# Soft MoE behind an RWKV recurrence on one core: slot sums kept in PSUM, a reordered last chunk, and expert 8 added onto replicated rows

## The chip, the cores and the metric

The kernel runs on one core of one Trainium2 chip. The metric is device time in microseconds (us) for one execution, lower is better. The kernel before took 137.22 us as the median of 13 runs (135.03 to 139.92).

## The reference, cut to what matters

Two stages follow each other. The first is a linear recurrence over 768 steps for each of 4 × 8 heads of width 48; the second takes its output as 3072 tokens of width 384, mixes them into 32 slots (8 experts, 4 slots each), runs each expert's two-layer network on its slots, and mixes the slots back.

```python
for t in range(S):                                   # per batch and head
    cur = einsum('bhd,bhe->bhde', u * k[t], v[t])
    y[t] = einsum('bhd,bhde->bhe', r[t], state + cur)
    state = w * state + einsum('bhd,bhe->bhde', k[t], v[t])
logits = x @ phi                                     # x = y, (3072, 384); phi (384, 32)
d = softmax(logits, axis=0);  slot_input = d.T @ x   # normalised over tokens
for e in range(8):
    slot_out[e] = relu(slot_input[e] @ w1[e]) @ w2[e]   # 384 -> 1024 -> 384
out = softmax(logits, axis=1) @ slot_out             # normalised over slots
```

## The kernel before, in words

The recurrence is computed in chunks. One chunk n is 256 tokens of one batch (two tokens per partition, index j), and there are twelve (nS = 12), three per batch. The order of instructions on every engine is the order of the code: nothing reorders it. What an engine waits for is derived from the tiles that instructions share.

For a chunk, SP loads k, r and v (`load`, L65, three DMAs of 384 KB, four buffers each, issued three chunks ahead). POOL multiplies r and k by powers of w (`mults`, L209, L211) and k by u (L212), two chunks ahead; chunk 0 has this on DVE (L205 to L207). ACT copies r into a PSUM tile rp (`r_copy`, L232), and DVE multiplies k·u by it (`kur`, L238), sums it (`dsum`, L249) and scales v (`dmul`, L256, tile dv). PE transposes r and k (`trans`, L269) and ACT copies them back (L272). `att` (L287) forms the 128 × 128 products of a chunk in two halves j = 0, 1, each in two PSUM banks at_p0 and at_p1, and DVE masks them into at_s (L292). The output y of the chunk accumulates in PSUM from three sources: the diagonal (`y_open`, L302), the state (`inter`, L314, for each half g) and the masked products (`intra`, L354). `state` (L327, L332) and `st_next` (L341) advance the state twice per chunk. ACT copies y to x_t (L365).

Routing follows one chunk behind: `xt` transposes x (L379, L381), `lg` forms logits (L417), `expo` takes exponentials (L426). `disp` (L437), two chunks behind, multiplies x and a column of ones by them into a PSUM tile s_p, which is also the tile of the state products, and DVE adds the result to un_a in SBUF (L441, L443). For each pair of chunks `lexp_t` and `rowsum` (L451 to L461) make the transposed weights LexpT and the reciprocals of their row sums. After the last chunk `last_routing` (L386) does both halves of the routing, un_a is divided by its sums (L533, L535, tile unsiT), and the experts follow in two groups of four (x = 0, 1): `up` (L552, L557, L559), `turn` (transposes of h, L567, L571) and `down` (L578), all with four experts side by side on 32 rows or columns of PE. The expert outputs so_p are copied (L591), replicated onto four groups of 32 rows by a matmul with a selection matrix idrep (L594), and copied again (L595, so_r). Twelve blocks of output follow: matmuls with LexpT (L607), a scaling by DVE or ACT (L613, L615) and a store from SP (L617, L619).

The weights w1 and w2 (25 MB in HBM) are loaded and cast by POOL's DMA queue (`load_w`, L170): 15 pieces of 768 KB, and the last expert's w2 in four of 192 KB. One piece is issued after each of chunks 0 to 8 (W_AT, L469), two inside chunk 9's `mults`, and the rest after them. `fill` issues matmuls whose result nobody reads.

Of the kernel before, what the change touches and what calls it, by code (L numbers as in the profile page):

```python
# [11 lines left out]
def kernel(  # L12
# [12 lines left out]
    nc = tc.nc  # L25
# [51 lines left out]

    wu_row = cst.tile([1, 2, Dm], f32, name="wu_row")
    for t, src in enumerate((w, u)):
        nc.sync.dma_start(out=wu_row[:, t, :], in_=src.flatten()[None, :])  # L80
# [8 lines left out]
    for n in range(3):  # L89
        load(n)  # L90
    warm = cst.tile([P, 1], f32, name="warm")
    nc.vector.memset(warm[:], 1.0)
# [31 lines left out]
    idrep = cst.tile([P, G, ES], bf, name="idrep")  # L124
    hT = cst.tile([P, 2, nF, P], bf, name="hT")
# [26 lines left out]
    un_a = cst.tile([P, (nM + 1) * ES], f32, name="un_a")  # L152
    unsiT = cst.tile([P, nM, 2, ES], bf, name="unsiT")
    csum_r = cst.tile([P, ES], f32, name="csum_r")
# [17 lines left out]
    with tc.tile_pool(name="wk", bufs=2) as wk, \  # L172
# [7 lines left out]
        nc.scalar.activation(out=warm[:], in_=warm[:], func=AF.Ln)  # L180
        nc.scalar.activation(out=logw[:], in_=wu_row[:, 0, :], func=AF.Ln)
        lw_p = ps.tile([P, Dm], f32, name="lw_p", tag="at_p0", padded_shape=[P, nP * P])
# [7 lines left out]
        nc.vector.tensor_copy(u_rep[:].rearrange("p h d -> p (h d)"), u_p[:])  # L190
        nc.vector.memset(idrep[:], 0.0)
        for c in range(XE):
            nc.vector.tensor_copy(idrep[c * ES:(c + 1) * ES, :, c * Spe:ES],
                                  ident[c * ES:(c + 1) * ES, None, c * ES:(c + 1) * ES - c * Spe]
                                  .to_broadcast([ES, G, ES - c * Spe]))

        def mults(n, inner=0):
# [6 lines left out]
            if n == 0:  # L204
                nc.vector.tensor_mul(kk[:, :, :, 0:D], jh(k_l), W_k[:])  # L205
                nc.vector.tensor_mul(rr[:, :, :, 0:D], jh(r_l), W_n[:])
                nc.vector.tensor_mul(ku, ku, u_b)  # L207
            else:
                nc.gpsimd.tensor_mul(rr[:, :, :, 0:D], jh(r_l), W_n[:])  # L209
                load_w(inner)  # L210
                nc.gpsimd.tensor_mul(kk[:, :, :, 0:D], jh(k_l), W_k[:])  # L211
                nc.gpsimd.tensor_mul(ku, ku, u_b)  # L212
# [9 lines left out]
        def r_copy(n, j):  # L222
# [3 lines left out]
            if n == 0 and j == 0:  # L226
                rp = ps.tile([P, H, D], f32, name="rp_first", tag="xl_p", padded_shape=[P, H, D + 8])
            else:
                rp = ps.tile([P, H, D], f32, name="rp") if n == 0 or j == 0 else s["rp"]
            s["rp"] = rp  # L230
            s["rps"] = s.get("rps", []) + [rp]
            nc.scalar.copy(rp[:], jh(loads[n][0])[:, j, :, :])  # L232

        def kur(n, j):
# [3 lines left out]
            nc.vector.tensor_mul(s["ku"][:, j, :, :], s["ku"][:, j, :, :], s["rps"][j][:])  # L238
# [7 lines left out]
        def dsum(n):  # L246
            s = sc[n]
            d = s["rp"][:].rearrange("p h d -> p (h d)")[:, 0:J * H].rearrange("p (j h) -> p j h", j=J)
# [26 lines left out]
        def att(n, j):  # L275
# [6 lines left out]
            at_p = [ps.tile([P, nP, P], f32, name=f"at_p{a}") for a in range(2)]  # L282
# [76 lines left out]
        def x_copy(n):  # L359
            x_t = wk3.tile([P, 2, Dm], bf, name="x_t")  # L360
            if n == nS - 1:
                nc.vector.tensor_copy(x_t[:, 0, :], sc[n]["y"][:, 0, 0:Dm])
                nc.scalar.copy(x_t[:, 1, :], sc[n]["y"][:, 1, 0:Dm])
            else:
                nc.scalar.copy(x_t[:], sc[n]["y"][:, :, 0:Dm])  # L365
            x_of[n] = x_t
            del sc[n]

# [3 lines left out]
        def xt(n):  # L372
# [3 lines left out]
            for g in range(2):  # L376
                for mi in range(nM):
                    o = (g * nM + mi) * P
                    nc.tensor.transpose(xl_p[:, o:o + P], x_of[n][:, g, mi * P:(mi + 1) * P], ident[:])  # L379
# [4 lines left out]
        def last_routing(n):  # L384
# [5 lines left out]
            for g in range(2):  # L390
                for mi in range(nM):
                    nc.tensor.transpose(bank[g][:, mi * P:(mi + 1) * P], x_of[n][:, g, mi * P:(mi + 1) * P], ident[:])
                if g == 0:
                    nc.vector.tensor_copy(xt_s[g][:], bank[g][:, 0:HW])
                else:
                    nc.scalar.copy(xt_s[g][:], bank[g][:, 0:HW])
            fill(2)
            for g in range(2):
                lg_p = bank[g][:, HW:HW + 2 * ES].bitcast(f32)
                for mi in range(nM):  # L400
                    nc.tensor.matmul(lg_p, xt_s[g][:, mi * P:(mi + 1) * P], phi_s[:, mi, :],
                                     start=(mi == 0), stop=(mi == nM - 1), skip_group_check=True)
                nc.scalar.activation(out=le[:, 2 * (n % 2) + g, :], in_=lg_p, func=AF.Exp)
# [4 lines left out]
        def lg(n):  # L408
# [10 lines left out]
            if n % 2 == 0:  # L419
                le_of[n // 2] = wk.tile([P, G, ES], bf, name="Lexp")  # L420
# [8 lines left out]
        def disp(n, s_p):  # L429
# [3 lines left out]
            for g in range(2):  # L433
                q = 2 * (n % 2) + g
                for mi in range(nM + 1):
                    lhs = ones[:] if mi == nM else x_of[n][:, g, mi * P:(mi + 1) * P]
                    nc.tensor.matmul(s_p[:, mi * ES:(mi + 1) * ES], lhs, le[:, q, :],  # L437
                                     start=(g == 0 and mi == 0), stop=(g == 1), skip_group_check=True)
            w = (nM + 1) * ES
            if n == 0:  # L440
                nc.vector.tensor_copy(un_a[:], s_p[:, 0:w])  # L441
            else:
                nc.vector.tensor_add(un_a[:], un_a[:], s_p[:, 0:w])  # L443
# [19 lines left out]
        def fill(count):  # L463
            pad = ps.tile([P, H, D], f32, name="pad", tag="rp")
            for _ in range(count):
                nc.tensor.matmul(pad[:].rearrange("p h d -> p (h d)"), ident[:], w1_all[:, 0, 0, 0:Dm],
                                 start=True, stop=True, skip_group_check=True)

        W_AT = [1] * 9 + [32] * 5  # L469
# [11 lines left out]
        for n in range(nS):  # L481
# [6 lines left out]
            s_now = ps.tile([P, nP * D2], f32, name="s_p")  # L488
            disp(n - 2, s_now)
            sc[n]["s"] = s_now  # L490
            trans(n + 1, "rr")
            if n == nS - 1:
# [157 lines left out]
```

The softmax here doesn't subtract the row's maximum and nothing guards it: scores larger than these inputs give would overflow.

## Time and profile before

| What | us |
|---|---|
| median of 13 runs | 137.22 |
| the profiled execution | 135.03 |
| its span on the core | 133.2 |
| PE busy | 99.1 (74%) |
| DVE busy | 97.9 (73%) |
| POOL busy | 78.6 (59%) |
| ACT busy | 77.2 (58%) |
| DMA: 31.78 MB moved | mean 238 GB/s |

In the profile PE is the matmul engine and PEld its weight loads; DVE, ACT and POOL are the vector, scalar and general engines; SP issues DMAs. A row such as `DVE at_s L292` names engine, tile written and line. An arrow `x<-y` reads "x written from y". In the chain of waits each line is a start, a length and what ran; in the timeline a bracket gives the idle time ahead of an instruction and who ended it. Bytes of the cast weights are counted as they arrive, in bf16.

### The profile page before, as it was taken

How to read it: one execution, taken by the hardware profiler on the slowest of the kernel's cores; microseconds unless marked ns; L12 is line 12 of the kernel's file. 1: busy time of each engine (PE TensorE's matmuls, PEld its weight loads, DVE VectorE, ACT ScalarE, POOL GpSimd, SP SyncE). 2: the span in 40 equal slices, each digit the busy share in tenths (PEclk: the TensorE clock that was granted, in tenths of full speed). 3: DMA queues.
4: the chain of work that ended last, by engine and by line, in shares of the span. 5: the costliest groups of instructions: out<-in, count | busy, mean ns of one | idle time of the engine just before them, and what ended most of it. 6: DMA issues, size and time to landing. Idle time of an engine off the chain costs nothing.

```text
span 133.2 us, 4106 instructions
## 1 busy us (share of the span) xinstructions
PE 99.1 (74%) x1727; PEld 69.4 (52%) x1727; DVE 97.9 (73%) x195; ACT 77.2 (58%) x130; POOL 78.6 (59%) x63
## 2 busy tenths in 40 slices
PE   0826898987589977997698868899868879779100
PEld 0325585865468665685467646686745545332000
DVE  6699997999787798868988996967895342277600
ACT  4848675776766577665948675765732422057500
POOL 5008999999999999189396894999370000000000
PEclk9999999999955599559959995555899999997555
DMA  1999999999999999999999999999999999119993
GB/s 22 319 323 325 325 325 290 244 261 260 232 267 240 259 248 239 238 231 247 184 211 290 192 243 281 170 198 207 208 206 203 206 202 200 20 45 412 406 406 153
DMA packets 51351, 31.78 MB, mean 238 GB/s; under 512 B 38386, under 2 KB 46836, under 8 KB 51332
## 3 DMA queue, kind: packets, MB, share of 16 engines
q0 software_dynamic: 11600, 12.63, 56.8%
q1 hardware_dynamic: 39316, 18.88, 49.2%
q8 instruction: 13, 0.21, 0.6%
q10 hardware_dynamic: 416, 0.00, 0.2%
q14 instruction: 6, 0.05, 0.1%
HBM read 39.38 MB, written 4.72 MB: 331 GB/s over the span
## 4 chain that ended last, share of the span: by engine, by line
DMA 26%; ACT 20%; PE 16%; DVE 15%; issue 9%; POOL 9%; DVEq 0%; ACTq 0%; POOLq 0%
DMA w_all<-in_moe_w_dram 14%; DMA r_l<-in_r_dram 7%; POOL w_all L170 5%; DVE at_s L292 5%; DMA out_dram<-o_s 5%; ACT t_kk L272 4%; ACT rp L232 4%; PE t_p L269 4%; DVE k_l L238 3%; ACT x_t L365 3%; ACT v_bf L219 3%; ACT xt_s L381 2%; PE at_p L287 2%; PE xl_p L379 1%; PE s_p L332 1%
## 5 line engine op out<-in xcount | busy, mean ns | idle before, releaser
L292 DVE TENSOR_TENSOR at_s<-at_p,mask 128x512 bf16<-128x512 f32 x48 | 30.9, 685 | 9.0 <-PE at_p L287 8.9
L209 POOL TENSOR_TENSOR rr<-r_l,W_n 128x768 bf16<-128x768 f32 x11 | 20.4, 1854 | 16.6 <-DMA r_l<-in_r_dram 16.5
L212 POOL TENSOR_TENSOR k_l<-k_l,u_rep 128x768 f32<-128x768 f32 x11 | 19.9, 1811 | 0.9
L211 POOL TENSOR_TENSOR kk<-k_l,W_k 128x768 bf16<-128x768 f32 x11 | 19.9, 1811 | 0.0
L232 ACT COPY rp<-r_l 128x384 f32<-128x384 f32 x23 | 11.2, 486 | 11.8 <-DVE k_l L238 11.6
L272 ACT COPY t_rr<-t_p 128x1024 bf16<-128x1024 bf16 x11 | 11.1, 1012 | 11.3 <-PE t_p L269 11.2
L287 PE MATMUL at_p<-t_rr,t_kk 64*64 64x128 bf16 x384 | 15.4, 269 | 2.7 <-DVE at_s L292 1.3
L170 POOL DMA_DIRECT2D w_all<-in_moe_w_dram x19 | 15.6, 830 | 2.1 <-DMA w_all<-in_moe_w_dram 2.1
L272 ACT COPY t_kk<-t_p 128x1024 bf16<-128x1024 bf16 x12 | 12.1, 1005 | 2.2 <-PE t_p L269 2.1
L332 PE MATMUL s_p<-v_bf,kk 64*128 64x96 bf16 x160 | 13.1, 238 | 0.0
L238 DVE TENSOR_TENSOR k_l<-k_l,rp 128x384 f32<-128x384 f32 x23 | 12.6, 549 | 0.6
L287 PEld LDWEIGHTS <-t_kk 64*64 64x64 bf16 x384 | 9.4, 131 | 6.5 <-issue 4.8
L332 PEld LDWEIGHTS <-kk 64*128 64x128 bf16 x160 | 9.6, 113 | 5.7 <-issue 5.7
L256 DVE TENSOR_TENSOR dv<-v_bf,rp 128x768 bf16<-128x768 bf16 x12 | 11.4, 953 | 1.5 <-ACT t_kk L272 0.5
L341 DVE TENSOR_TENSOR st<-s_p,wm 128x384 bf16<-128x384 f32 x20 | 11.0, 552 | 1.5 <-PE s_p L332 1.3
L269 PE MATMUL t_p<-ident,kk 128*128 128x128 bf16 x96 | 10.0, 267 | 2.6 <-DVE kk L205 2.6
L249 DVE TENSOR_REDUCE rp<-k_l 128x16 f32<-128x768 f32 x12 | 11.5, 958 | 0.3
L365 ACT CAST x_t<-y_p 128x768 bf16<-128x768 f32 x11 | 8.9, 805 | 3.4 <-PE y_p L354 3.4
L381 ACT COPY xt_s<-xl_p 128x768 bf16<-128x768 bf16 x11 | 8.8, 800 | 2.7 <-PE xl_p L379 2.7
L615 ACT ACTIVATE o_s<-o_p,rsum_r 128x384 f32<-128x384 f32 x12 | 6.4, 585 | 6.6 <-PE o_p L607 4.4
L354 PE MATMUL y_p<-v_bf,at_s 64*128 64x48 bf16 x384 | 9.8, 192 | 0.3 <-issue 0.3
L269 PEld LDWEIGHTS <-kk 128*128 128x128 bf16 x96 | 7.4, 120 | 5.0 <-DVE kk L205 3.7
(105 smaller groups left out, 177.9 us busy)
## 6 DMA issues: line engine op xcount, KB each, us to landing
w_all<-in_moe_w_dram POOLq DMA_DIRECT2D x15, 768.0 KB, 9.8
k_l<-in_k_dram SPq DMA_DIRECT2D x12, 384.0 KB, 6.0
r_l<-in_r_dram SPq DMA_DIRECT2D x12, 384.0 KB, 6.1
v_l<-in_v_dram SPq DMA_DIRECT2D x12, 384.0 KB, 9.0
out_dram<-o_s SPq DMA_DIRECT2D x11, 384.0 KB, 4.1
w_all<-in_moe_w_dram POOLq DMA_DIRECT2D x4, 192.0 KB, 20.4
out_dram<-o_s SPq DMA_DIRECT2D x2, 192.0 KB, 1.9
phi_f<-in_moe_phi_dram POOLq DMA_DIRECT2D x1, 48.0 KB, 4.7
```

The source lines that it names most:

```text
L170: nc.gpsimd.dma_start(out=dst, in_=src)
L209: nc.gpsimd.tensor_mul(rr[:, :, :, 0:D], jh(r_l), W_n[:])
L211: nc.gpsimd.tensor_mul(kk[:, :, :, 0:D], jh(k_l), W_k[:])
L212: nc.gpsimd.tensor_mul(ku, ku, u_b)
L232: nc.scalar.copy(rp[:], jh(loads[n][0])[:, j, :, :])
L238: nc.vector.tensor_mul(s["ku"][:, j, :, :], s["ku"][:, j, :, :], s["rps"][j][:])
L269: nc.tensor.transpose(t_p[:, q, :, j, :], s[nm][:, j, 2 * q:2 * q + 2, :].rearrange("p h d -> p (h d)"), ident[:])
L272: nc.scalar.copy(t_s[:], t_p[:])
L287: nc.tensor.matmul(at_p[a][g * HF:(g + 1) * HF, q, :], kT[sl, q, g, j, :], rT[sl, q, g, :, :].rearrange("p j c -> p (j c)"), start=True, s ...
L292: nc.vector.tensor_mul(s["at"][:, a, j, :, :], at_p[a][:], mask[:, j, None, :].to_broadcast([P, nP, P]))
L332: nc.tensor.matmul(s_p[:, q * D2:(q + 1) * D2], s["kk"][sl, j, 2 * q:2 * q + 2, :].rearrange("p h d -> p (h d)"), s["v"][sl, j, 2 * q:2 * ...
L365: nc.scalar.copy(x_t[:], sc[n]["y"][:, :, 0:Dm])
```

## The change

1. The first chunk's loads are issued ahead of the two small loads of w and u, which move from SP to ACT's DMA queue; the first activation table is loaded right behind them. 30 unread matmuls (`spin`) are put around PE's first products. The copy u_rep moves behind the products of chunk 0, and idrep is built much later.
2. `disp` accumulates over all chunks in one PSUM tile (rpun, which also holds rp) and the additions into un_a go. The sums stay unscaled: unsiT is a plain copy, and the reciprocal of the sums (csum_r, turned to a column csum_c by a matmul) scales so_r at the end instead, in two halves, DVE's and ACT's.
3. POOL issues two weight pieces after chunk 5 instead of one.
4. The last chunk has its own order: the second half of `att` uses the bank t_p beside at_p0, `intra` stands ahead of the second `inter`, the second transposes and row sums (`last_weights`, `last_sums`) move between `turn` and `down`, and y is copied into two tiles, ACT's and DVE's.
5. Expert 8 is left out of `down(1)`. Its h is copied into four row groups (hL), and its eight matmuls add onto the replicated rows sr_p. The memsets of hT (POOL before) and hL are on DVE.

```diff
+    load(0)
-        nc.sync.dma_start(out=wu_row[:, t, :], in_=src.flatten()[None, :])
+        nc.scalar.dma_start(out=wu_row[:, t, :], in_=src.flatten()[None, :])
+    nc.scalar.activation(out=warm[:], in_=warm[:], func=AF.Ln)
...
+        rpun = ps.tile([P, 512], f32, name="rpun")
+        un_p = rpun[:, Dm:Dm + (nM + 1) * ES]
+        rp_v = rpun[:, 0:Dm].rearrange("p (h d) -> p h d", h=H)
...
-                    nc.tensor.matmul(s_p[:, mi * ES:(mi + 1) * ES], lhs, le[:, q, :],
-                                     start=(g == 0 and mi == 0), stop=(g == 1), skip_group_check=True)
-                nc.vector.tensor_add(un_a[:], un_a[:], s_p[:, 0:w])
+                    nc.tensor.matmul(un_p[:, mi * ES:(mi + 1) * ES], lhs, le[:, q, :],
+                                     start=(n == 0 and g == 0 and mi == 0), stop=(n == nS - 1 and g == 1),
+                                     skip_group_check=True)
...
-        W_AT = [1] * 9 + [32] * 5
+        W_AT = [1] * 5 + [2] + [1] * 3 + [32] * 5
...
+        n = nS - 1
+        att(n, 0)
+        disp(n - 2)
+        xt(n - 1)
+        y_open(n)
+        sc[n]["s"] = ps.tile([P, nP * D2], f32, name="s_p")
+        state(n, 0)
+        att(n, 1)
+        inter(n, 0)
+        lg(n - 1)
+        expo(n - 1)
+        fill(4)
+        st_next(n, 0)
+        intra(n)
+        inter(n, 1)
+        x_last(n, 0)
+        x_last(n, 1)
+        fill(1)
+        disp(n - 1)
+        last_routing(n)
+        disp(n)
+        fill(3)
...
+        nc.vector.tensor_copy(unsiT[:], un_p[:, 0:nM * ES].rearrange("p (m s) -> p m s", m=nM)[:, :, None, :]
+                              .to_broadcast([P, nM, 2, ES]))
+        nc.vector.reciprocal(csum_r[:], un_p[0:1, None, nM * ES:(nM + 1) * ES].to_broadcast([1, G, ES]))
...
+        nc.vector.memset(hT[:], 0.0)
+        nc.vector.memset(hL[:], 0.0)
...
         up(0)
         up(1)
         turn(0)
+        selection()
+        last_weights()
         down(0)
         turn(1)
+        last_sums()
         down(1)
...
+        nc.vector.tensor_copy(so_b[:], so_p[:])
+        nc.tensor.matmul(sr_p[:], idrep[:].rearrange("p g t -> p (g t)"), so_b[:], start=True, stop=False,
+                         skip_group_check=True)
+        for fi in range(nF):
+            nc.tensor.matmul(sr_p[:], hL[:, fi, :, :].rearrange("p g t -> p (g t)"), w2_all[:, E - 1, fi, :],
+                             start=False, stop=(fi == nF - 1), skip_group_check=True)
+        nc.vector.tensor_scalar_mul(so_r[:, 0:Dm // 2], sr_p[:, 0:Dm // 2], csum_c[:])
+        nc.scalar.activation(out=so_r[:, Dm // 2:Dm], in_=sr_p[:, Dm // 2:Dm], func=AF.Copy, scale=csum_c[:])
```

## The prediction

> **What bounds the kernel now.** I read the page first (slices, chain), then the chain in order of time, three-microsecond windows, the timeline of the end and POOL's waits. The slices say that the 16 DMA engines are busy from 3 to 113 us and that no compute engine is:
>
> ```profile
> PE 99.1 (74%) x1727; PEld 69.4 (52%) x1727; DVE 97.9 (73%) x195; ACT 77.2 (58%) x130; POOL 78.6 (59%) x63
> ...
> DMA  1999999999999999999999999999999999119993
> ```
>
> The chain in order of time (start, length, what) shows which transfer ends last, and what follows it:
>
> ```profile
> 72.49 9.20 DMA r_l<-in_r_dram
> ...
> 96.50 18.93 DMA w_all<-in_moe_w_dram
> 115.43 0.04 issue
> 115.47 0.50 PE so_p L578 x2
> 115.99 0.57 DVE so_b L591
> 116.56 0.04 issue
> 116.60 0.34 PE sr_p L594
> 116.96 0.57 DVE so_r L595
> 117.57 0.61 PE o_p L607 x8
> ```
>
> The last slice of expert 8's w2 lands at 115.43; two matmuls, a copy, a matmul and a copy later, at 117.57, the output starts. From there to 133.2 the DMA writes 4.72 MB at about 413 GB/s; nothing there changes, so I price everything at the first output matmul. But compute is nearly as late. In the timeline the second `down` starts at 113.54 and sits idle only 0.33 us before its last pair:
>
> ```profile
> 107.99 2.77 PE L552 MATMUL h_p<-w_all,unsiT 128*32 128x512 bf16 x48 [0.35 <-DVE rsum_r L461]
> ...
> 113.54 2.41 PE L578 MATMUL so_p<-w_all,hT 128*32 128x384 bf16 x32
> 115.47 0.09 PEld L578 LDWEIGHTS <-hT 128*32 128x32 bf16 x1 [0.33 <-issue]
> ```
>
> So two chains end together: transfers (A) and compute (B). A saving counts only as far as both have it. The windows (last two columns: DMA share, GB/s) show how full A is:
>
> ```profile
> 39.00:42.00 3.00, 2.58 (x31) 2.02 (x30) 2.77 (x5) 2.73 (x4) 2.98 (x3) 0.50 1.11 210
> 63.00:66.00 3.00, 1.60 (x55) 1.26 (x54) 2.78 (x5) 3.00 (x5) 0.84 (x2) 1.00 0.98 189
> 84.00:87.00 3.00, 2.57 (x30) 2.24 (x27) 2.92 (x7) 2.03 (x5) 2.92 (x3) 0.50 0.97 156
> 93.00:96.00 3.00, 3.00 (x68) 2.50 (x67) 2.89 (x5) 2.06 (x3) 1.36 (x2) 0.82 1.12 207
> ```
>
> Loads of r, k, v alone run at 325 GB/s (9 to 21 us), weights alone at 207 (counted as bf16). Only 63 to 66 and 84 to 87 lie below both: 3 × (1 − 156/207) = 0.74 us of empty engines in the second, and about 1.0 in the first, whose mix of loads and weights would run near 280 (the rate of 69 to 72). POOL issues the weights between its products, and it waits for loads:
>
> ```profile
> POOL rr L209 <- DMA r_l<-in_r_dram: 16.5, 5, 7.6
> ```
>
> **What the Trainium skill says.** "DMA: Bandwidth & Descriptors", section Queues, rings and completion order: each engine goes round-robin, packet by packet, over the queues that have work, so a load beside a weight crawls. The trace agrees: at 39 to 42 us, with v_l issued at 37.54 still outstanding, the rate is that of weights alone. "PSUM — Partial Sum Buffer", section PSUM bank collisions raise a hardware error: two engines may not touch one bank and quadrant at once, reads included. The trace agrees: ACT's x_t copy (L363, 103.64) starts only when DVE's copy of the other half of y_p (L362, 103.05 for 0.56) is done. "VectorE: DVE Perf Modes", section Zero memsets can be issued as uint32: a memset takes a cycle per element; here 128 take 0.17 us, 384 take 0.38, so 0.82 ns each.
>
> **The start.** SP issues two wu_row DMAs at 0.74 and 1.15 ahead of k_l at 1.44; now k_l goes first: A −0.70. ACT issues wu_row instead, and its w_pd issues (0.89 for two) move between the two table steps, so logw goes from 3.23 to about 4.2 and W_k from 5.47 to 6.0–6.4 (the second table load, 1.28, now follows logw in the open). That costs nothing, because kk of chunk 0 (L205) waits in DVE's queue behind u_rep, idrep's memset and its four copies until 8.25. Without these it starts near 7.3. u_rep (0.56) returns ahead of ku. First kur: 11.08 to about 10.7, B −0.4. If POOL needed W_n earlier this would show, but POOL starts at 10.39 on a load. The spins lie in PE's idle time before 9.29; no row shows 30 such matmuls, the pads' 0.16 to 0.24 each bound them at 7 us, of which at most 1 us could push the transposes; I take 0.
>
> **Slot sums.** The 11 adds and one copy into un_a (0.28 each, 3.3 us of DVE) go. In the loop they are not in the chain by name: it runs over ACT's copies, kur and at_s, and DVE waits for PE's at_p right after them. Bounds for ten chunks: 0 and −2.8; I take 0. disp now shares rp's bank, so its first weight load waits for DVE's dv, which stands ahead of st (today's wait) in DVE's queue: no later than now. r_copy waits for disp, but t_rr's copy ahead of it waits for the transposes behind disp anyway. Queued behind disp: those transposes.
>
> **The extra weight at n=5.** POOL issues a second 768 KB weight at 53.96, ahead of rr for chunk 8, which waits for its load until 57.10 anyway: 0.94 us hidden. It adds no bytes, only order. One weight is 786 KB, 3.84 us at 205 GB/s. For: the hole at 63 to 66 fills, A up to −1.0. Against: r_l of chunk 9, landing at 65.6 now, waits behind one or two weights more, 3.9 to 7.7 us. ku of chunk 9 ends at 71.08 and is first used by kur at 76.97: slack 5.9. I take 0, with −1.0 and +1.8 (7.7 − 5.9) as ends.
>
> **The last chunk (B).** Today att(11,0) starts at 97.10 and `up` at 107.99: 10.9 us. New order from the same start and rows: disp(9), xt, y_open and state fill PE until 99.5, where today's PE waits for at_s; second att to 99.9; at_s on DVE to 101.25; st_next to 101.8; intra from 101.4, inter to 102.35; x copies one after the other (0.48, 0.56) to 103.4; transposes and copies to 104.15; logits, exp to 104.7; disp to 105.1; one copy (0.36) replaces add, reciprocal and product (0.29 + 0.35 + 0.36), and the last LexpT and row sums leave: `up` at 105.55. B −2.4, with −1.5 and −3 as ends.
>
> **Up, turn, down (B).** Counted from `up`. DVE first does csum_r (128 elements; rows of 4 and 32 give 0.18 and 0.35, so 0.9) and the memsets of hT and hL (1024 and 512 words: 0.9 + 0.45), so h_s is 0.34 later than PE needs it; two transposes 0.28; `selection` 0.9 hides under down(0); hL copy 0.2 and nine small matmuls 0.35 ahead of down(1), which starts at 6.5 where it is 5.55 now. Its 24 matmuls run three abreast (1.5, to 8.0), so_b 0.6, then nine full ones (0.33 + 8 × 0.16 = 1.6), to 10.2. so_r's halves, 0.4 each, are not parallel: in the built program ACT's half waits for DVE's (both read sr_p): to 11.15. Today 9.58. B +1.57. POOL's memset of hT (1.83) leaves a queue that is empty by then: 0.
>
> **The tail (A).** After the last landing: 0.04 + two matmuls 0.50 + 0.02 + 0.40 + 0.03 + 0.40 + 0.05 = 1.44, where it is 2.14. A −0.70.
>
> **Sum.** A: −0.70 − 0.70 = −1.40. B: 105.55 − 0.4 + 11.15 = 116.3 against 117.57, −1.25. The later decides: −1.25. The profiled execution took 135.03 us, 133.2 of it span; it is the fastest of the 13. Applied to the median 137.22: 136.0. What made the slower ones slow I can't see; a lower TensorE clock would weigh on B.
>
> **Rivals.**
> Likeliest, 0.42: 136.0, own range 135.2 to 136.9.
> Faster, 0.25: the extra weight fills the hole without hurting chunk 9 (A −2.4), and the missing adds shorten ten chunks by 0.1 each (B −2.3): 134.9, down to 133.8. For it: DVE is the busiest engine of the loop beside ACT. Against: the adds are not in the chain.
> Slower, 0.18: the extra weight starves POOL. rr of chunk 9 starts 7 us late; the loads then all finish early, and a weight every 5.4 us of products (three times 1.81) can't fill engines that need one every 3.84. One gap of 2.7 us opens near 85: A −1.40 + 2.7 = +1.3, 138.5. It decides once chunk 9's load is over 5.9 us later than now. For it: POOL already waits there five times. Against: 16.5 us of such waits leave the engines full today.
> No change, 0.15: the new order gains only 1.2 in the last chunk, because ACT's copies and not PE's waits set it; B −0.05: 137.2.
>
> **Numbers.** The measurement tells about 0.5% (0.7 us) from no change. Faster by more: most of the first case and all of the second, 0.60; same 0.21; slower 0.19. Range 134.0 to 138.2.
>
> **What would show it.** First k_l issue near 0.74; `up` 8.5 us after the last att(·,0) starts; first output matmul 1.4 to 1.5 us after the last weight lands; so_r's ACT half behind DVE's; no hole near 63 us. Wrong if chunk 9's rr starts after 71 or DMA share falls under 0.9 near 85.

## The result, and the profile after

| | kernel before | kernel after |
|---|---|---|
| median, us | 136.68 (48 runs, 134.72 to 140.10) | 138.51 (11 runs, 137.3 to 141.5) |
| the profiled execution, us (its span) | 135.03 (133.2) | 138.13 (136.4) |
| ratio after to before | | 1.0154, 95% interval 1.0111 to 1.0198 |

Slower by 1.5%, where −0.9% was forecast. Ratios compare undisturbed executions with undisturbed ones, so a median over all executions can stand a little off its ratio, and the one execution of each kernel that has a profile was a disturbed one in e5, e12 and i1 below.

The page of the kernel after, engines, chain shares, and the group of rr on POOL (GpSimd):

```profile
PE 105.9 (78%) x1759; PEld 75.6 (55%) x1759; DVE 97.4 (71%) x186; ACT 77.7 (57%) x131; POOL 77.0 (56%) x62
...
POOL 32%; issue 21%; PE 18%; DMA 9%; ACT 8%; DVE 4%; SPq 2%; POOLq 0%; DVEq 0%; ACTq 0%
...
L214 POOL TENSOR_TENSOR rr<-r_l,W_n 128x768 bf16<-128x768 f32 x11 | 20.6, 1877 | 20.1 <-DMA r_l<-in_r_dram 20.0
```

POOL, which has 44% of the span free, now holds the largest share of the chain, and its waits for r_l have grown from 16.5 to 20.0 us. The timeline of POOL in the kernel after shows where (start, length, what, and in brackets the idle time ahead of it):

```profile
55.41 1.81 POOL L170 DMA_DIRECT2D w_all<-in_moe_w_dram  x2
58.21 1.81 POOL L214 TENSOR_TENSOR rr<-r_l,W_n 128x768 bf16<-128x768 f32 x1 [0.99 <-DMA r_l<-in_r_dram]
...
63.62 0.94 POOL L170 DMA_DIRECT2D w_all<-in_moe_w_dram  x1
73.76 1.80 POOL L214 TENSOR_TENSOR rr<-r_l,W_n 128x768 bf16<-128x768 f32 x1 [9.20 <-DMA r_l<-in_r_dram]
```

Two weights are issued at 55.41 and a third at 63.62; rr of chunk 9 starts at 73.76, where it was 65.62: 8.1 us later. A window of the kernel after (POOL's column is 0.00; DMA share and GB/s last), and its DMA queues in the same three microseconds (packets, MB, share of the engines; q0 carries the weights, q1 the loads), show who had the engines meanwhile:

```profile
69.00:72.00 3.00, 2.72 (x28) 2.01 (x26) 2.39 (x6) 1.93 (x4) 0.00 (x0) 0.50 1.25 204
```

```profile
q0 software_dynamic: 533, 0.41, 86.3%
q1 hardware_dynamic: 535, 0.20, 38.8%
```

The total of 204 GB/s is also that of weights alone, but the loads do move: one packet of a load (384 bytes) goes for each packet of a weight (768 bytes). So loads get a third of the bytes, about 68 GB/s where they have 325 alone, and one load of 393 KB takes 5.8 us. SP had issued this r_l at 56.98: it was over 15 us under way. In e1 below, with one weight, it is issued at 56.95 and rr starts at 66.25; the weight's own part of the delay is then 7.5 us.

Chunk 9's ku then reaches kur at 79.25 instead of 76.97, and the last chunk's first scores start at 99.05 instead of 97.10. But DVE waits for ku only 0.51 us:

```profile
79.25 0.55 DVE L243 TENSOR_TENSOR k_l<-k_l,rpun 128x384 f32<-128x384 f32 x1 [0.51 <-POOL k_l L217]
```

DVE itself was late, because PE was. The same window in the kernel after, in the kernel before and in e1 (PE's busy time and matmuls first; third from the end is the granted clock, the share of its full speed that PE gets):

```profile
67.00:80.00 13.00, 12.55 (x180) 9.25 (x178) 9.01 (x16) 7.13 (x12) 6.14 (x5) 0.50 1.18 244
```

```profile
67.00:80.00 13.00, 10.77 (x226) 7.94 (x223) 11.54 (x22) 9.22 (x15) 11.01 (x8) 0.88 1.21 235
```

```profile
67.00:80.00 13.00, 9.45 (x237) 7.44 (x234) 11.57 (x20) 9.46 (x17) 10.63 (x7) 1.00 1.23 232
```

From first scores to first scores, a chunk takes 7.19 us in e1 at full clock (71.71 to 78.90); in the kernel after chunk 7 takes 9.12 (65.63 to 74.75), 1.6 more than before, and no product of chunk 9 is used in it. So in this profile the late load is 0.5 us of the 1.95, at most the 1.0 that chunk 8 loses, and the rest goes with the half clock.

The timeline from the last chunk to `up`:

```profile
107.72 0.36 DVE L544 CAST unsiT<-rpun 128x192 bf16<-128x192 f32 x1 [0.87 <-PE rpun L445]
107.99 0.93 DVE L546 RECIPROCAL csum_r<-rpun 1x128 f32<-1x128 f32 x1
...
108.98 1.26 PE L594 MATMUL h_p<-w_all,unsiT 128*32 128x512 bf16 x20 [0.81 <-DVE csum_r L546]
```

`up` waits not for unsiT, which it reads, but for csum_r, which it doesn't: both read the PSUM bank of rpun, and the h_p tiles take its place. `up` at 108.98 is 9.93 us after the last chunk's start (10.89 before, 8.45 forecast). The end, in the same view:

```profile
117.17 1.46 PE L645 MATMUL sr_p<-w_all,hL 128*128 128x384 bf16 x8
...
118.66 0.42 DVE L647 TENSOR_SCALAR so_r<-sr_p,csum_c 128x192 bf16<-128x192 f32 x1 [1.71 <-PE sr_p L645]
...
119.12 0.42 ACT L648 ACTIVATE so_r<-sr_p,csum_c 128x192 bf16<-128x192 f32 x1 [4.35 <-DVE so_r L647]
...
119.59 0.85 PE L660 MATMUL o_p<-so_r,LexpT 32*64 32x384 bf16 x16 [0.96 <-ACT so_r L648]
```

The eight matmuls of the eighth expert run in one stretch: the last weight, landed at 116.84, was there before them. So compute (chain B) ended last, at 119.59 against 117.57, and the difference adds up: +1.95 at the last chunk's start, −0.96 to `up`, +1.03 from `up` to the output = +2.02. From there to the landing of the last store it took 15.7 us, against 14.6; the kernels below took 14.6 to 15.9, and I have no cause for that 1.1. The last weight, too, landed late: 116.84 against 115.43, though the first load was issued at 0.74 as forecast.

To see where transfers (chain A) lost time, I worked out from the packets of the trace, stretch by stretch, how much transfer time is missing: the length of the stretch less the loads' bytes at 325 GB/s and the weights' at 205. I call it the gap. From 17 to 25 us it is 0.51 us before and 1.36 after; from 54 to 60 it is 0.33 and 1.51. The second difference is not the extra weight's: e1, with one weight, has 1.19 there, and e2, with two, 0.35.

### The profile page after: what moved, and what is told of

It is laid out like the page before. It is cut to its first block, busy times and chain, and to the rows that moved or that the text cites. A ratio compares the mean times of both kernels' runs of the same rounds, so it can differ in the third digit from the quotient of the medians.

```text
span 136.4 us, 4158 instructions
## 1 busy us (share of the span) xinstructions
PE 105.9 (78%) x1759; PEld 75.6 (55%) x1759; DVE 97.4 (71%) x186; ACT 77.7 (57%) x131; POOL 77.0 (56%) x62
## 4 chain that ended last, share of the span: by engine, by line
POOL 32%; issue 21%; PE 18%; DMA 9%; ACT 8%; DVE 4%; SPq 2%; POOLq 0%; DVEq 0%; ACTq 0%
POOL kk L216 12%; POOL k_l L217 9%; POOL rr L214 6%; DMA out_dram<-o_s 5%; POOL w_all L170 5%; DMA r_l<-in_r_dram 4%; SPq L72 2%; PE so_p L623 2%; PE h_p L594 2%; PE t_p L274 2%; ACT x_t L367 2%; PE pad L470 1%; ACT t_kk L277 1%; PE s_p L338 1%; DVE k_l L243 1%
## 5 line engine op out<-in xcount | busy, mean ns | idle before, releaser
L298 DVE TENSOR_TENSOR at_s<-at_at_p,mask 128x512 bf16<-128x512 f32 x47 | 30.3, 685 | 11.3 <-PE at_at_p L293 11.2
L237 ACT COPY rpun<-r_l 128x384 f32<-128x384 f32 x23 | 11.2, 486 | 12.4 <-DVE k_l L243 12.0
L293 PE MATMUL at_at_p<-t_rr,t_kk 64*64 64x128 bf16 x376 | 15.2, 274 | 2.5 <-DVE at_s L298 1.2
L338 PE MATMUL s_p<-v_bf,kk 64*128 64x96 bf16 x160 | 13.9, 247 | 0.0
L338 PEld LDWEIGHTS <-kk 64*128 64x128 bf16 x160 | 10.2, 117 | 5.9 <-issue 5.9
L243 DVE TENSOR_TENSOR k_l<-k_l,rpun 128x384 f32<-128x384 f32 x23 | 12.6, 549 | 1.2 <-POOL k_l L217 0.5
L261 DVE TENSOR_TENSOR dv<-v_bf,rpun 128x768 bf16<-128x768 bf16 x12 | 11.4, 953 | 1.1
L254 DVE TENSOR_REDUCE rpun<-k_l 128x16 f32<-128x768 f32 x12 | 11.5, 955 | 0.3
L274 PE MATMUL t_p<-ident,kk 128*128 128x128 bf16 x96 | 10.7, 280 | 0.0
L320 PE MATMUL y_p<-st,t_rr 128*128 128x96 bf16 x80 | 8.7, 248 | 1.6 <-DVE st L347 1.5
L224 ACT CAST v_bf<-v_l 128x768 bf16<-128x768 f32 x12 | 9.9, 829 | 0.0
L274 PE MATMUL t_p<-ident,rr 128*128 128x128 bf16 x88 | 9.7, 278 | 0.3 <-POOL rr L214 0.3
```

The costliest lines, as they stand in the source:

```text
L254: nc.vector.tensor_reduce(d, s["ku"], axis=mybir.AxisListType.X, op=ALU.add)
L274: nc.tensor.transpose(t_p[:, q, :, j, :], s[nm][:, j, 2 * q:2 * q + 2, :].rearrange("p h d -> p (h d)"), ident[:])
L293: nc.tensor.matmul(at_p[a][g * HF:(g + 1) * HF, q, :], kT[sl, q, g, j, :], rT[sl, q, g, :, :].rearrange("p j c -> p (j c)"), start=True, s ...
L298: nc.vector.tensor_mul(s["at"][:, a, j, :, :], at_p[a][:], mask[:, j, None, :].to_broadcast([P, nP, P]))
L338: nc.tensor.matmul(s_p[:, q * D2:(q + 1) * D2], s["kk"][sl, j, 2 * q:2 * q + 2, :].rearrange("p h d -> p (h d)"), s["v"][sl, j, 2 * q:2 * ...
```

## The experiments

Two questions. First, what made it slower: the theory (T1) is the slower rival of the prediction, the second weight at chunk 5; its rivals are csum_r ahead of `up` and the longer steps behind it (T2 in the recorded texts), and the transfers that landed late. Second, once T1 stood: why undoing the weight doesn't bring the forecast gain. Ratios are to the kernel before, with 95% intervals; each kernel had 22 executions unless another number is given.

| kernel | ratio | interval |
|---|---|---|
| e1, after with one weight | 1.0015 | 0.9984 to 1.0047 |
| e2, before with two weights (6) | 1.0149 | 1.0082 to 1.0215 |
| e3, after with late csum_r | 1.0060 | 1.0022 to 1.0099 |
| e4, e1 and e3 together | 1.0017 | 0.9986 to 1.0049 |
| e5, e4 with the old start (6) | 1.0168 | 1.0098 to 1.0238 |
| e6, e4 with five buffers (6) | 1.0112 | 1.0039 to 1.0185 |
| e7, after with five buffers | 1.0083 | 1.0044 to 1.0122 |
| e8, e4 without the eighth expert's change | 1.0065 | 1.0024 to 1.0105 |
| e9, e4 without spins | 0.9973 | 0.9940 to 1.0005 |
| e10, before with the new start (6) | 1.0109 | 1.0042 to 1.0176 |
| e11, before with the eighth expert's change | 0.9964 | 0.9920 to 1.0008 |
| e12, before with both (6) | 1.0225 | 1.0147 to 1.0302 |
| h1, e10 with squarings on POOL (14) | 1.0028 | 0.9964 to 1.0092 |
| h2, e9 with squarings on POOL | 0.9928 | 0.9893 to 0.9963 |
| h3, e12 with squarings on POOL (14) | 0.9983 | 0.9938 to 1.0028 |
| h4, e9 with the old start | 1.0018 | 0.9968 to 1.0067 |
| i1, h2 with two weights | 1.0038 | 1.0005 to 1.0071 |
| i2, h2 with spins | 0.9984 | 0.9946 to 1.0022 |

**e1: the second weight taken out of the kernel after.**

```diff
-        W_AT = [1] * 5 + [2] + [1] * 3 + [32] * 5
+        W_AT = [1] * 9 + [32] * 5
```

> The changed kernel with one weight piece after chunk 5, as before (W_AT), and nothing else undone. Theory T1 (the second piece keeps chunk 9's loads waiting, POOL starts chunk 9's rr at 73.8 in place of 65.6, and chunks 9 to 11 start 1.95 us late): rr of chunk 9 back near 65 to 66, last chunk's att at 96.7 to 97.2, first output matmul at 117.0 to 117.4, time 0.2 to 0.6 us under the kernel before. Theory T2 (the delay is made in the new last chunk and the longer up, turn and down): last att moves by less than 0.5 us and the time stays 1.3 us or more over the kernel before.

Measured 1.0015: the loss of 1.5% is gone. rr of chunk 9 starts at 66.25. The gain that was expected on top didn't come: the output follows the last weight, which lands at 116.55, by 1.49 us.

**e2: the second weight alone, put into the kernel before** (the same line the other way round).

> The kernel before with the second weight piece after chunk 5 and nothing else. T1: rr of chunk 9 at 72 to 75, last att 1.5 to 2 us late, time 1.5 to 2.5 us over the kernel before. T2: within 0.5 us of the kernel before, since nothing at the end is changed.

Measured 1.0149, which is the whole of the loss. POOL's timeline in this kernel repeats the pattern:

```profile
53.08 1.82 POOL L170 DMA_DIRECT2D w_all<-in_moe_w_dram  x2
...
62.35 0.94 POOL L170 DMA_DIRECT2D w_all<-in_moe_w_dram  x1
71.18 1.80 POOL L209 TENSOR_TENSOR rr<-r_l,W_n 128x768 bf16<-128x768 f32 x1 [7.89 <-DMA r_l<-in_r_dram]
```

So T1 holds from both sides as to the time: the weight is enough for the loss, and without it there is none. As to the path it holds only in part. In this profile DVE waits 0.68 us for POOL's ku at chunk 11, the last chunk starts 0.75 us late (97.85), and then it takes 13.38 us to `up` instead of 10.89, with the granted clock at 0.50 for 10 of them.

**e3: the reciprocal of the kernel after moved off `up`'s way.** The bank is released by a copy of 32 sums, and csum_r is made in `selection`.

```diff
-        nc.vector.reciprocal(csum_r[:], un_p[0:1, None, nM * ES:(nM + 1) * ES].to_broadcast([1, G, ES]))
+        csum_x = cst.tile([1, ES], f32, name="csum_x")
+        nc.vector.tensor_copy(csum_x[:], un_p[0:1, nM * ES:(nM + 1) * ES])
...
         def selection():
+            nc.vector.reciprocal(csum_r[:], csum_x[0:1, None, :].to_broadcast([1, G, ES]))
```

> The changed kernel with csum_r's 0.93 us reciprocal taken out from between unsiT and up: a copy of the 32 sums (about 0.1) stands there, and the reciprocal follows in selection, under down(0). Both theories: up starts 0.8 us sooner after unsiT. T1: that is a part of the loss only, first output matmul at 118.7 to 118.9, the time still 1.0 to 1.5 us over the kernel before. T2: the time falls by 0.8 us and up to 1.3 with what follows it, to within 0.6 us of the kernel before.

Measured 1.0060, 0.9% under the kernel after. Its timeline, both weights still in:

```profile
104.19 0.36 DVE L544 CAST unsiT<-rpun 128x192 bf16<-128x192 f32 x1 [0.87 <-PE rpun L445]
104.47 0.17 DVE L547 COPY csum_x<-rpun 1x32 f32<-1x32 f32 x1
...
104.70 0.83 PE L596 MATMUL h_p<-w_all,unsiT 128*32 128x512 bf16 x12
```

The copy takes 0.17 us where the reciprocal took 0.93, and `up` comes 8.07 us after the last chunk's first scores. That the time falls while the second weight is in, and (next) not when it is out, fits compute as the later chain. This profile, though, is of the fastest of the 22 executions (135.56 us), and in it the second weight does no harm: rr of chunk 9 starts at 67.68, DVE doesn't wait for POOL in chunks 9 to 11, and the output follows the last weight by 1.49 us. So two weights do not starve chunk 9 in every execution.

**e4: both.**

> Both edits: one weight piece after chunk 5, and csum_r late. If the two losses add (1.95 and 0.8), the compute chain ends about 2.8 us earlier than in the changed kernel, and the transfers (116.2 for the first output matmul) decide: 1.0 to 1.5 us under the kernel before. If transfers were the real end already, no more than 0.3 us better than the run with one weight piece alone.

Measured 1.0017, no better than e1. The timeline of its end says why:

```profile
114.81 1.14 PE L647 MATMUL sr_p<-w_all,hL 128*128 128x384 bf16 x6
116.46 0.48 PE L647 MATMUL sr_p<-w_all,hL 128*128 128x384 bf16 x2 [0.52 <-DMA w_all<-in_moe_w_dram]
...
117.91 0.52 PE L662 MATMUL o_p<-so_r,LexpT 32*64 32x384 bf16 x8 [0.96 <-ACT so_r L650]
```

Here A decides: PE waits for the last weight, landed at 116.42, and the output starts 1.49 us later. The tail is as forecast (1.44), but the weight lands 1.0 us later than before instead of 0.7 earlier: the second question.

**e5 and e6: does the early start vanish in four load buffers?** e5 puts the old start back into e4 (w and u on SP ahead of the first load). e6 gives r and k five buffers, and the cast v and x two in place of three.

```diff
-            t = loads[n][x]
+            t = loads[n][x] = ld.tile([P, H, J, D], f32, name=("r_l", "k_l", "v_l")[x], bufs=(5, 5, 4)[x])
...
-            load(n + 3)
+            load(n + 3, (2,))
+            load(n + 4, (0, 1))
```

> The kernel with one weight per chunk and the late reciprocal, but with the start of the kernel before: SP issues the rows w and u ahead of the first load, and the table load stands where it stood, so the first load goes out near 1.4 us instead of 0.74. If the four load buffers give the early start back between 17 and 25 us (SP then waits for a buffer sooner and longer), the last weight lands where it did (116.4 us of a profile), the gap at 17 to 25 us shrinks from 1.3 us of lost transfer to about 0.5, and the time is 136.9 (within 0.3). If the early start reaches the end of the transfers, the time rises by 0.6 to 0.8, to 137.6.

> The kernel with one weight per chunk and the late reciprocal, with five buffers for r and k in place of four, their loads issued four chunks ahead, the load of v three ahead as before, and two buffers in place of three for the cast v and x. If four buffers give the early start back, and cause other gaps in the transfers, the gap at 17 to 25 us goes, the last weight lands 0.7 to 1.2 us sooner (115.2 to 115.7), and since it ends last there, the time falls to 135.7 to 136.2. If SP's waits for buffers cost no transfer (the queue holds enough), it stays at 136.9, and the end is set by the rate at which weights and loads share the engines.

Neither came as written. The gap at 17 to 25 us was 1.14 in e5 and 1.31 in e6: it is there with the old start and with five buffers, so the four buffers don't make it. The times, 1.0168 and 1.0112, rest on four and two executions; they are above e4, and for e6 against its own profile, whose last weight lands at 115.11. I leave e6's time unexplained.

**e7: five buffers in the kernel after, two weights left in.**

> The kernel after, with two weights at chunk 5, with the five buffers alone added. If the extra weight delays chunk 9 because its loads wait for a buffer, rr of chunk 9 starts near 66 to 68 us again instead of 73.8 and the time falls to 136.5 to 137.2. If the extra weight delays it by taking the DMA engines while the loads are already issued, rr of chunk 9 still starts after 71 and the time stays within 0.5 of 138.5.

Measured 1.0083, 0.7% under the kernel after, with intervals that touch: between the two answers. rr of chunk 9 starts at 68.25, as the first one said, in a profile of the fastest execution (135.69 us). That the fifth buffer does it is not shown. Its r_l was issued at 54.31, ahead of the second weight (55.76), where the kernel after issues it behind (56.98 and 56.34); but e3, with four buffers, issues it at 53.91 and has rr at 67.68, and e2 at 53.10 with rr at 71.18.

**e8: e4 without the eighth expert's change.**

```diff
+            for group in ((0, 1, 2), (3,)) if x == 1 else ((0, 1, 2, 3),):
                 for fi in range(nF):
-                for c in range(XE - x):
+                    for c in group:
...
-        for fi in range(nF):
-            nc.tensor.matmul(sr_p[:], hL[:, fi, :, :].rearrange("p g t -> p (g t)"), w2_all[:, E - 1, fi, :],
-                             start=False, stop=(fi == nF - 1), skip_group_check=True)
```

> The kernel with one weight per chunk and the late reciprocal, with the eighth expert undone: down(1) runs experts 5 to 7 and then the eighth into so_p, and so_b and the replication follow the last weight; no hL. Where transfers end last, the step from the last weight's landing to the first output matmul goes from 1.49 us back to about 2.1 to 2.3, and the time rises by 0.6 to 0.8, to 137.6. If compute ends last anyway, the time stays at 136.9 or falls by up to 0.3, since the two copies into hL and its memset go.

Measured 1.0065, 0.5% over e4. In its timeline the copy and the replication are behind the last weight again, which landed at 115.28:

```profile
115.32 0.48 PE L620 MATMUL so_p<-w_all,hT 128*32 128x384 bf16 x2 [0.23 <-DMA w_all<-in_moe_w_dram]
...
116.45 0.32 PE L639 MATMUL sr_p<-so_b,idrep 128*128 128x384 bf16 x1 [0.65 <-DVE so_b L638]
...
117.73 0.85 PE L654 MATMUL o_p<-so_r,LexpT 32*64 32x384 bf16 x8 [0.96 <-ACT so_r L642]
```

2.45 us from landing to output against e4's 1.49. The step works where A decides.

**e9: e4 without the 30 spin matmuls.**

```diff
-        spin(12)
...
-        spin(18)
```

> The kernel with one weight per chunk and the late reciprocal, without the 30 spin matmuls at the start. In the profiles of after and of every kernel made from it the first 16 KB instruction fetch stands at 16.0 to 18.5 us instead of 20.4, and a gap of 1.1 to 1.4 us of lost transfer follows in 17 to 25 us, where before has 0.5. If the spins' instructions bring the fetch forward and that makes the gap, the fetch goes back to about 20, the gap falls to 0.5 to 0.7, and the time falls by 0.5 to 0.8, to 136.2. If the spins have nothing to do with it, the gap stays above 1.1 and the time at 136.9 (within 0.3).

Measured 0.9973, 0.4% under e4 with intervals that overlap; the fetch came at 18.7 us and the gap was 0.98. That the fetch makes the gap fell with e10, where it comes at 21.7 and the gap is 2.1.

**e10, e11, e12: the start and the eighth expert's change alone in the kernel before.**

```diff
+    load(0)
...
-        nc.sync.dma_start(out=wu_row[:, t, :], in_=src.flatten()[None, :])
+        nc.scalar.dma_start(out=wu_row[:, t, :], in_=src.flatten()[None, :])
+    nc.scalar.activation(out=warm[:], in_=warm[:], func=AF.Ln)
...
-    for n in range(3):
+    for n in range(1, 3):
         load(n)
```

> The kernel before with the new start alone: load(0) first, the rows w and u on ScalarE, the table load behind them. If the earlier start reaches the end where transfers end last, the time is 0.5 to 0.8 below before, ratio 0.995. If it is given back between 17 and 25 us by something that comes with the start itself, the time stays at that of before, ratio 1.000, and the gap there grows from 0.5 to 1.2 us.

> The kernel before with the eighth expert's change alone: hL, down(1) over experts 5 to 7, so_b and the replication ahead of the last weight, the eighth expert's eight matmuls onto sr_p; so_r still copied whole by DVE. Transfers and compute end together before, so if the prediction's step is right the time from the last weight's landing to the first output matmul falls from 2.14 us to 1.5 and the time by 0.5 to 0.8, ratio 0.995. If compute ends last, it stays within 0.3 of before: the up to down steps get the two hL copies and the memset, 0.5 us, and lose expert 8's second group, about as much.

> The kernel before with both: the new start and the eighth expert's change, nothing else. If the two gains on the transfer chain stand and compute isn't in the way, the time is 1.0 to 1.4 below before, ratio 0.991, faster than either kernel. If compute ends last, as before's 10.9 us from the last chunk's first scores to the first up allow, 0.3 to 0.6 below, ratio 0.997. If the start is given back, ratio 0.995.

e11 did what was expected (0.9964; 1.18 us from landing to output, with so_r copied whole). e10 and e12 missed on the far side: 1.0109 and 1.0225. The new start by itself makes the kernel before slower. Its gap at 17 to 25 us is 2.10 us, the largest of all; the windows of e10 and, below, of the kernel before:

```profile
21.00:22.00 1.00, 1.00 (x43) 0.94 (x43) 0.90 (x2) 0.44 (x2) 1.00 (x1) 1.00 0.53 146
22.00:23.00 1.00, 0.95 (x21) 0.71 (x13) 1.00 (x3) 0.59 (x1) 0.98 (x3) 1.00 0.53 116
```

```profile
21.00:22.00 1.00, 0.64 (x15) 0.46 (x17) 0.71 (x2) 0.77 (x1) 1.00 (x2) 1.00 1.14 310
22.00:23.00 1.00, 1.00 (x24) 0.62 (x15) 0.56 (x1) 0.63 (x2) 0.98 (x2) 1.00 1.03 263
```

In e10 SP's waits name what holds the next load, the k of chunk 5, until 21.20 (19.06 before): `rp`, chunk 1's row sums on DVE.

```profile
SPq L72 <- DVE rp L250: 2.7, 1, 2.7
```

DVE is late from chunk 0 on. First the timeline of e10, then that of the kernel before:

```profile
8.90 0.96 DVE L206 TENSOR_TENSOR kk<-k_l,W_k 128x768 bf16<-128x768 f32 x1
...
9.91 2.49 POOL L210 TENSOR_TENSOR rr<-r_l,W_n 128x768 bf16<-128x768 f32 x1 [7.11 <-DMA r_l<-in_r_dram]
...
10.65 2.57 DVE L208 TENSOR_TENSOR k_l<-k_l,u_rep 128x768 f32<-128x768 f32 x1
```

```profile
8.28 0.96 DVE L205 TENSOR_TENSOR kk<-k_l,W_k 128x768 bf16<-128x768 f32 x1
...
10.02 0.95 DVE L207 TENSOR_TENSOR k_l<-k_l,u_rep 128x768 f32<-128x768 f32 x1
10.39 2.25 POOL L209 TENSOR_TENSOR rr<-r_l,W_n 128x768 bf16<-128x768 f32 x1 [7.59 <-DMA r_l<-in_r_dram]
```

The same product on DVE takes 0.95 us when it starts before POOL's rr, and 2.57 when it starts after it; POOL's rr takes 2.25 instead of 1.81 when it is second. The Trainium skill says so: "SBUF — State Buffer", section SBUF: two separate sides, has DVE operations with two SBUF inputs and GpSimd operations take one shared pair of ports as an exclusive lock, for the whole instruction. The traces agree, with 1.6 us as the loser's price on DVE: in e10, e3 and e4 DVE's product ends 0.8 us after POOL's rr does. Why is DVE behind? w_pd's issue on ACT moved from 0.91 to 1.65 us, behind w and u and behind loads already under way. It lands at 6.0 instead of 3.6; its seven squarings, which started at 4.52 in their turn, now start at 6.13 after 1.53 us of waiting, take 1.34 us, and stand on DVE ahead of chunk 0.

**h1, h3, h2: only the squarings moved from DVE to POOL**, in e10, e12 and e9.

```diff
-        nc.vector.tensor_mul(w_pd[:], w_pd[:], w_pd[:])
+        nc.gpsimd.tensor_mul(w_pd[:], w_pd[:], w_pd[:])
```

> Start-only (the kernel before with the new start) with the seven squarings of w_pd on GpSimd, which is idle until 9.9 us, instead of VectorE. If w_pd's late landing is what costs, VectorE starts chunk 0's kk near 7.9 instead of 8.9, its k_l takes 0.95 us and not 2.57, chunk 5's k issues near 18.5 to 19 us, the gap at 17 to 25 us falls from 2.1 to 0.5 to 0.9, and the ratio to before from 1.011 to 0.995 to 1.000. If the early loads themselves cost, the gap and 1.011 stay.

> The kernel before with the new start, the eighth expert's change and the squarings on GpSimd, nothing else. Without the squarings on GpSimd it stood at 1.0225. If w_pd's late landing was the cause, the gap at 17 to 25 us falls from 1.9 to 0.5 to 0.9 and the ratio to 0.990 to 0.997, at or below the eighth expert's change alone (0.996). If the early loads themselves cost, it stays above 1.01.

> The kernel with one weight per chunk, the late reciprocal and no spins, with the squarings of w_pd on GpSimd too. If w_pd's landing holds chunk 0, its kk starts near 6.3 us instead of 7.5, the gap at 17 to 25 us falls from 1.0 to about 0.5, the last weight lands 0.3 to 0.7 us sooner, and the ratio goes from 0.997 to 0.991 to 0.995, faster than both kernels. If not, it stays at 0.997.

h1 went from 1.0109 to 1.0028, h3 from 1.0225 to 0.9983, with the early loads unchanged. The timeline of h1, where DVE is first at the ports again:

```profile
9.79 0.95 DVE L208 TENSOR_TENSOR k_l<-k_l,u_rep 128x768 f32<-128x768 f32 x1
10.09 2.32 POOL L210 TENSOR_TENSOR rr<-r_l,W_n 128x768 bf16<-128x768 f32 x1 [1.03 <-DMA r_l<-in_r_dram]
```

So late squarings and the lock they lead into, not the early loads, cost most of e10's and e12's loss; clear of the intervals this is in h3 alone, and the two profiles of e10 and h1 don't show it (the output starts at 118.94 and 119.06). But the gaps fell only to 1.35 and 1.08, not below 0.9, and neither ratio beats its twin without the new start (1.000 and 0.9964): the 0.70 us still don't show. h2 is the fastest of all, 0.9928, below both kernels; its chunk 0 starts at 6.28 instead of 7.52. Its gap, though, is 1.42, so it isn't by a smaller gap that it gained.

**h4: e9 with the old start.**

> The kernel with one weight per chunk and the late reciprocal, with the start of the kernel before and no spins. With the spins it stood at 1.017 with a gap of 1.14 us at 17 to 25; with the new start and no spins at 0.997 with 0.98. If the spins make part of the gap (0.6 us), the gap here falls to 0.5 and the ratio to 0.992 to 0.997. If the spins have no part, 1.005 to 1.017 stays.

Measured 1.0018, gap 0.88: between the two answers. Against e5 it says that the spins cost 1.5%, against e9 that the new start is worth 0.5%, give or take 0.9 and 0.6. So in this form of the kernel the new start doesn't hurt, as it does in the kernel before; the copies into idrep, which delay chunk 0 there, are gone here. e5's 1.0168 I trust less for it.

**i1 and i2: the second weight and the spins, each put back into h2.**

> The fastest kernel so far (one weight per chunk, late reciprocal, no spins, the squarings of w_pd on GpSimd: 0.993 of before) with two weights at chunk 5 as in the change. If the extra weight starves chunk 9's loads whatever the rest is, rr of chunk 9 starts after 70 us instead of 65.9 and the ratio rises by 1.0 to 1.5 per cent, to 1.003 to 1.008. If it was only the combination with the late chunk 0, the ratio stays at 0.993 to 0.996.

> The fastest kernel so far with the 30 spin matmuls put back, which is the kernel with one weight per chunk and the late reciprocal (1.002 of before) with the squarings on GpSimd. If the squarings carry the gain, 0.993 to 0.996; if the spins cost most of it, 0.998 to 1.002. In the trace chunk 0's k_l on VectorE starts near 8.7 us, over 1 us ahead of GpSimd's rr of chunk 1, and takes 0.96 us in either case.

i1: 1.0038, 1.1% over h2. Its profile is of a longer execution (138.82 us, the median is 136.92), with POOL's line as in the kernel after:

```profile
72.09 1.80 POOL L212 TENSOR_TENSOR rr<-r_l,W_n 128x768 bf16<-128x768 f32 x1 [8.28 <-DMA r_l<-in_r_dram]
```

Here the starving shows plainly: DVE waits 1.33 us for POOL's ku at chunk 9 and 0.99 at chunk 11, and the chunks before these take 9.42 and 8.52 us with the clock at half for only 0.8 and 1.7 us of them. None of the 15 profiles with one weight has such a wait in chunks 9 to 11.

i2: 0.9984, 0.6% over h2. Most of h2's gain over e4 is then the spins' going; the squarings' part (i2 against e4, −0.3%) is within the intervals.

## Why the prediction was wrong, by its own steps

- **The extra weight at n=5, the step that failed.** It was taken at 0, with −1.0 and +1.8 us as ends; it costs 1.1 to 1.5%, which is 1.5 to 2.0 us: +1.49% in before (e2), 1.39% between after and e1, 1.1% between i1 and h2 (0.4% between e3 and e4, within their intervals). The working of the bad end held for the load: 7.7 us was the bound for two weights, 7.5 were measured between e1 and after, and rr of chunk 9 started after 71, which the prediction had named as a sign of being wrong. What misled was the argument for 0, that the weight is issued inside a wait of POOL's. The issue is hidden; the packets behind it are not. That 5.9 us of slack swallow the load's delay all but 2.3 us, as kur of chunk 9 seems to say by coming 2.3 us later, is luck in this profile: 0.51 us of that is a wait for POOL, the rest is a slower PE. The reading "the rate is that of weights alone" at 39 to 42 us hid the same thing as at 69 to 72: loads move there too, with 0.06 of 0.63 MB. And the hoped-for gain didn't come: with two weights the last one lands no earlier (116.84 against 116.55 in e1, 115.80 in e2 against 115.43 in before).
- **The rival's gap near 85 was wrong.** The share there didn't fall (87 to 90 us is 1.00), and the added gaps are spread out, at 17 to 25, 54 to 60 and 78 to 84. The 138.5 came by compute, B, and not by A as that rival had it, and on another median of the kernel before (136.68, not 137.22): that the figure fits is luck.
- **The last chunk, −2.4: right as a mechanism, −0.96 measured in after.** `up` came 9.93 instead of 8.45 after the last chunk's first scores. Two things are missing. One is csum_r, which the prediction put beside `up` ("DVE first does csum_r") and which stood ahead of it by the shared bank: 0.75 us between e1 (8.83) and e4 (8.08); with it moved, e3 and e4 have −2.8. The other, 1.1 us between after and e1, is the granted clock, 0.50 in after from 101 to 104 us and full in e1; four pads that fill(4) puts ahead of intra take 1.28 us there. At half clock in that chunk e8, h2 and i1, too, have 9.8 to 10.2.
- **Up, turn, down, +1.57: +1.03 measured**, less the csum_r that had moved ahead; the halves of so_r ran one behind the other, as said.
- **The tail, −0.70: right.** 1.49 us from landing to output in e3 and e4 against 1.44 forecast, and 0.5 and 0.4% in time (e8 against e4, e11 against before, both in the forecast direction, each with an interval that just includes zero).
- **The start, −0.70: wrong.** k_l is issued at 0.74 as said, and 0.7 us are won by 4 us. Up to 25 us 3.6 us are missing in before, and 3.5 to 4.1 in all kernels with the new start but e10, e12 and h1, which have more. Of the late w_pd the prediction saw the issue and not the landing: it followed the late rows into W_k, not into DVE's queue, where the squarings stand first. W_k came earlier, not later (5.18 us). Chunk 0's kk at 7.40 and its kur at 10.79 are as forecast (7.3 and 10.7), but by luck: the squarings set them.
- **The spins, 0: likely wrong in size.** Without them the time fell in three pairs, by 0.4, 0.6 and 1.5%; only the last, which rests on e5, is clear of the intervals.
- **Slot sums, 0: it stands.** No run tried them alone, but at full clock a chunk takes 7.21 us in before (73.52 to 80.73) and 7.19 in e1, without the additions.

What stays open: by which path the second weight costs its 1.1 to 1.5% in most executions (waits of DVE for POOL of 0.5 to 2.3 us show in the profiles of after, e2 and i1, next to none in e3 and e7; half clock adds to it in after and e2); what makes the gap at 17 to 25 us where DVE wins the ports (after, e6, e9 and h2 have 0.98 to 1.42 us, though up to 23 us no load waits longer for a buffer than in before; SP's single issues take up to 2.4 us instead of 1.1), and so where the early start's 0.7 us go in the better kernels; and by which path the spins cost time.

## What to carry to other kernels

A transfer that is issued inside a wait is free only if nothing that is waited for stands behind it in the engines: price the bytes, not the issue, and count the slack of the next load against two or three such transfers. Before a difference between two profiles is given to the change, compare the granted clock in that stretch. When two chains end together, take a part out of each and one alone back in before you believe the sum; here each of two repairs hid the other's worth. And when a small transfer moves behind a large one, follow its landing into the queue of every engine that reads it.

## What was not expected of the hardware

- **A race for SBUF's shared ports, decided by hundredths of a microsecond.** DVE's k_l of chunk 0 and POOL's rr of chunk 1 start 0.17 us apart in the profile of after (9.73 and 9.90: DVE first, 0.96 us), 0.02 apart in e9 (9.85 and 9.87: 0.96), and the other way round in e3 and e4 (9.79 behind 9.77: 2.59; 9.77 behind 9.71: 2.56). Each kernel has one trace, so whether executions of one kernel fall on both sides is not shown.
- **A load beside queued weights gets packet for packet, a third of the bytes.** From 69 to 72 us of after 535 packets of loads went with 533 of weights, in e2 from 62 to 68 us 1,108 with 1,065. With three weights queued, r_l's 393 KB landed over 15 us after their issue.
- **The granted clock sets the pace of a chunk.** Where it is full throughout, a chunk takes 7.18 to 7.20 us (31 chunks of 16 kernels); where it is 0.50 for 8 us or more, 8.7 to 9.1 us, with one weight (8.73 in before, 9.12 in i2) as with two (9.12 in after).
- **With the spins TensorE's granted clock is lower, not higher.** In three pairs its mean over the executions compared is lower with the spins: 0.821 against 0.838 (e4, e9), 0.822 against 0.838 (e5, h4), 0.807 against 0.831 (i2, h2). With two weights it is lower as well: 0.794 against 0.828 (after, e1), 0.805 against 0.828 (e2 and before with it), 0.825 against 0.831 (i1, h2). Whether this is how they cost time was not shown; within one kernel, executions with a lower mean clock took hardly longer (0.02 us for 0.01 of clock, pooled over 14 kernels).
